# Cosformer attention into a top-1 mixture of experts: two lasting row tiles, a later one-hot table, earlier expert reads and copied row numbers

## The chip, the cores and the metric

The kernel runs on one core of one Trainium2 chip. The metric is the device time of one execution in microseconds, the median over runs; lower is better. Engines are named as the profile names them: PE (TensorE), DVE (VectorE), ACT (ScalarE), POOL (GpSimd), SP (SyncE). Transfers are issued by SP and POOL; the profile gives them as queue q1 (SP's) and q0 (POOL's).

## What is computed

```python
q_p = phi(q); k_p = phi(k)          # relu(x)*cos, relu(x)*sin: 64 -> 128 features
kv  = einsum('bhsf,bhsd->bhfd', k_p, v);  z = k_p.sum(axis=2)
x   = einsum('bhsf,bhfd->bhsd', q_p, kv) / (q_p . z + 1e-6)   # 8 x 8 x 576 x 64
x   = x.transpose(0, 2, 1, 3).reshape(4608, 512)
e_idx  = argmax(x @ w_gate)         # 8 experts, the best one alone
gate_w = softmax(x @ w_gate)[e_idx]; eom = sigmoid(x @ w_output_gate)
out[mask e] = gate_w * eom[:, e] * (relu(x[mask e] @ w1[e]) @ w2[e])   # 512 -> 1024 -> 512
```

## The kernel before

**Attention.** 36 units i = 0..35 of 128 rows, nine to a group g = 0..3 of two batches. PE multiplies a unit by the finished KᵀV (`q_mm`, L542, L547), ACT and DVE put it into a tile `u` (L554, L556), and after every second unit and after a group's last one `q_out` follows: DVE takes the reciprocal of the denominators (`rc`, L566, L567), POOL writes the divided rows as f16 into the group's `xr` tile (L576), and DVE (POOL for some) makes the gate products `gl` (L593) and sums them to gate numbers `glog` (L600). `xr` comes from a pool with two buffers, so group g takes the buffer of group g-2.

**Routing.** `route` (L607 to L667) is a generator that gives way at each `yield`; `step()` runs it on to the next one. It finds each row's expert (`ei`, L626), writes the one-hot table `oh` (L629), counts ranks within experts by six or ten small matmuls on PE (`rk`, L637, L639), and makes row numbers `di` and weights `meta` on DVE (to L666). Group 3 is routed in two halves, of slots 0 to 3 and 4 to 8 of the group. `scatter(g, c)` (L669) is POOL's: it copies `meta` behind the rows (L675), and an indirect DMA (L678) writes 128 rows to the table `xs`, sorted by expert, in HBM.

**Experts.** `xs` is worked off in 39 slots j of 128 rows of one expert; the first 8 (EARLY) take rows of groups 0 to 2 only. SP reads a slot (`fetch`, L811; `xg`, 8 buffers); PE turns it (`x_tr`, L824), ACT or DVE copies the turned tile (`xts`, L848); PE multiplies by the first matrix (`layer1`, L885, into `hp`), ACT applies relu (`hs`, L893); `h_tr` turns that again, by PE (L866) and a DVE copy (`hts`, L868) or, for slots 18 to 36, by a DMA of SP (L861); `products` (L907) multiplies by the second matrix into one of two halves of a PSUM tile `yps`; `output` scales it on DVE (`ysb`, L918, 5 buffers), and POOL writes 128 rows to the output by an indirect DMA (L922), the row numbers being those in `xg` (j < 8) or in `sidx`. `expert(j)` (L871) reads the expert's number into a register of PE's sequencer, by a load and two register instructions.

**Order.** The schedule is by hand: each engine runs its instructions in the order in which the code writes them, and waits there. Before the main loop stand slots 0 to 2 and the scatters of group 3; the main loop (L1152) does in iteration j: `h_tr(j-1)`, `x_tr(j+1)`, `expert(j+1)`, `layer1(j)`, `layer2` of slot j-1 (j-2 for the slots turned by DMA), the fetch of slot j+5. POOL also loads the experts' matrices (`load_w`, L238 and L241, 1 MB each in f16), those of ranks 4 to 7 in iterations 4 to 11. POOL's DMAs hold eight semaphores in turn (DMASW0 to DMASW7 in the listings below), so that an instruction that waits for one waits for a landing.

Of the kernel before, what the change touches and what calls it, by code (L numbers as in the profile page):

```python
# [13 lines left out]
I32 = mybir.dt.int32  # L14
U8 = mybir.dt.uint8
U16 = mybir.dt.uint16
# [6 lines left out]
def kernel(  # L23
# [237 lines left out]
    GP.memset(onesf[:], 1.0)  # L261
    valid = constp.tile([P, NL], U8, name="valid")
    sidx = constp.tile([P, NL], I32, name="sidx")
    GP.memset(sidx[:], BIG)
    nlate = constp.tile([P, 1], I32, name="nlate")
    perm = constp.tile([P, E, E], F32, name="perm")
# [7 lines left out]
    if True:  # L274


        zt = wk.tile([P, XW], U16, name="zt", tag="zt", bufs=1)
        DVE.memset(zt[:], 0)
        DVE.memset(zt[:, DM:DM + 2].bitcast(I32), BIG)

        def idle_mms(ps, n):

            z = zt[:, 0:DM].bitcast(F16)
            for _ in range(n):
                PE.matmul(ps, z[:, 0:P], z, start=True, stop=True)
# [324 lines left out]
        def route(g, glog, xrows, c0=0, c1=GC):  # L610


            m = c1 - c0
            lg = glog[:, c0:c1, 0:8]
            im8 = iota8m[:].unsqueeze(1).to_broadcast([P, m, E])
            lmax = small(f"lmax@{g}_{c0}", [P, m])
            DVE.tensor_reduce(lmax[:], lg, AX.X, ALU.max)
            lmb = lmax[:].unsqueeze(2).to_broadcast([P, m, E])
            sh = small(f"sh@{g}_{c0}", [P, m, E])
            DVE.tensor_tensor(sh[:], lg, lmb, ALU.subtract)  # L620
            om = small(f"oh@{g}_{c0}", [P, m, E])

            DVE.tensor_tensor(om[:], lg, lmb, ALU.is_equal)
            DVE.tensor_tensor(om[:], om[:], im8, ALU.mult)
            ei = small(f"ei@{g}_{c0}", [P, m])
            DVE.tensor_reduce(ei[:], om[:], AX.X, ALU.min)  # L626
            oh16 = oh16s[(m, g % 2)]
            oh = oh16[:, 0:m, :]
            DVE.tensor_tensor(oh, im8, ei[:].unsqueeze(2).to_broadcast([P, m, E]),  # L629
                              ALU.is_equal)  # L630
            yield
            ex = small(f"ex@{g}_{c0}", [P, m, E])
            ACT.activation(ex[:], sh[:], AF.Exp)

            rk_t = ptr.tile([P, 512], F32, name=f"rk{g}_{c0}", tag="tr")
            rk = rk_t[:, 0:(m + 1) * E].rearrange("p (c e) -> p c e", e=E)
            PE.matmul(rk, u16[:], oh16[:], start=True, stop=False)  # L637
            for c in range(m):
                PE.matmul(rk[:, c + 1:, :], ones16[:],  # L639
                          oh16[:, c:c + 1, :].to_broadcast([P, m - c, E]),  # L640
                          start=False, stop=(c == m - 1))
            ds_ = small(f"ds@{g}_{c0}", [P, m, E])
            DVE.tensor_tensor(ds_[:], rk[:, 0:m, :],
                              base[:].unsqueeze(1).to_broadcast([P, m, E]), ALU.add)
            DVE.tensor_tensor(base[:], base[:], rk[:, m, :], ALU.add)
            yield
            og = small(f"og@{g}_{c0}", [P, m, E])
            DVE.tensor_tensor(og[:], oh, glog[:, c0:c1, 8:16], ALU.mult)
            den = small(f"den@{g}_{c0}", [P, 2, m])
            DVE.tensor_reduce(den[:, 1, :], og[:], AX.X, ALU.add)  # L650
            yield
            ACT.activation(den[:, 1, :], den[:, 1, :], AF.Exp, scale=-1.0)
            yield
            DVE.tensor_tensor(ds_[:], ds_[:], oh, ALU.mult)
            df = small(f"df@{g}_{c0}", [P, m])
            DVE.tensor_reduce(df[:], ds_[:], AX.X, ALU.add)
            di = small(f"di@{g}_{c0}", [P, m], I32, bufs=5)
            DVE.tensor_copy(di[:], df[:])
            DVE.tensor_reduce(den[:, 0, :], ex[:], AX.X, ALU.add)
            DVE.tensor_scalar_add(den[:, 0, :], den[:, 0, :], 1e-9)  # L660
            meta = small(f"meta@{g}_{c0}", [P, m, 2], bufs=5)
            DVE.tensor_scalar(meta[:, :, 0].bitcast(I32), id0[:, c0:c1], float(2 * S * g),
                              None, ALU.add)
            DVE.scalar_tensor_tensor(den[:, 1, :], den[:, 1, :], 1.0, den[:, 0, :],
                                     ALU.add, ALU.mult)
            DVE.reciprocal(meta[:, :, 1], den[:, 1, :])  # L666
            scat[g] = (di, meta, xrows, c0, c1)  # L667
# [246 lines left out]
        def output(j):  # L914
            xg = xgs.pop(j)
            yp = yps[0][:, j % 2, :]
            ysb = fsb.tile([P, DM], F32, name=f"ysb{j}", tag="ysb", bufs=5)
            DVE.tensor_scalar(ysb[:], yp, xg[:, DM + 2:DM + 4].bitcast(F32),  # L918
                              None, ALU.mult)
            idx = (xg[:, DM:DM + 2].bitcast(I32) if j < EARLY  # L920
                   else sidx[:, j - EARLY:j - EARLY + 1])
            d = GP.indirect_dma_start(  # L922
                out=out[:, :],
                out_offset=bass.IndirectOffsetOnAxis(ap=idx, axis=0),
                in_=ysb[:], in_offset=None,
                bounds_check=N - 1, oob_is_err=False)
            tc.declare_no_dep(d.ins, group="so", reason="distinct rows")
            tc.add_to_no_dep_group("so", d.ins)
# [89 lines left out]
        for i, (b, c) in enumerate(units):  # L1018
            g = b // 2
            n = i % 9  # L1020
            if n == 0:
                glog = wk.tile([P, GC, 16], F32, name=f"glog{g}", tag="glog")
                xrows = wk.tile([P, GC, XW], U16, name=f"xr{g}", tag="xr")
                scd = 0
            if c % 2 == 0:
                u = u2[(g + n // 2) % 2]
# [29 lines left out]
            if 30 < i < NU - 2:  # L1056
                if i == 31:
                    ip = pkv.tile([P, 2, 512], F32, name="idle1", tag="kvp")
                idle_mms(ip[:, 0, :], 4)
            if i == NU - 3:  # L1060
                x_tr(0)
# [62 lines left out]
        late = late_table()  # L1124


        for j in range(3):
            expert(j)
        layer1(0, pkv.tile([P, 2, 512], F32, name="hp0", tag="kvp"))
        for x in range(4):  # L1130
            scatter(NG - 1, x)
# [3 lines left out]
        layer1(1)  # L1135
        h_tr(0)
        layer1(2)
        step()
        h_tr(1)
        expert(3)  # L1140
        x_tr(3)
        x_copy(3)
        step()
        products(0)
        products(1)
        step(2)
        assert not pending
        for x in range(4, GC):
            scatter(NG - 1, x)
# [2 lines left out]
        for j in range(3, NMAIN + 1):  # L1152
# [4 lines left out]

            for _ in range(3 if j < 5 else 0):
                next(late, None)
            if j + 1 < NMAIN:  # L1160
                expert(j + 1)
            if j < NMAIN:
                layer1(j)
            if j + 1 < EARLY:
                x_copy(j + 1)
            for m in (j - 2, j - 1):
                if (m in BY_DMA) == (m == j - 2):
                    if j == NMAIN - 1 and m == j - 1:

                        h_tr(j)  # L1170
                    layer2(m)
            if j == 6:
                late_valid()
            for jj in {4: [8, 9]}.get(j, [j + 5]):
                if 4 <= j and jj < NSLOT:
                    fetch(jj)
# [47 lines left out]
```

## Time and profile before

| what | value |
|---|---|
| median of 3 runs | 329.85 us (328.68 to 330.81) |
| profiled execution | 327.69 us, its span 326.0 us |
| PE busy | 290.2 us (89%) |
| DVE busy | 197.5 us (61%) |
| ACT busy | 157.1 us (48%) |
| POOL busy | 140.6 us (43%) |
| moved by DMA | 71.82 MB, mean 220 GB/s |
| queue q1, queue q0 | 43.1% and 38.6% of 16 DMA engines' span |

The profile is of one execution. Its span runs from the first instruction to the last; the execution's own time is 1.7 us longer. Shares are means over the whole span: attention ends at about 153 us, and the main loop runs from 171 us to the end, so the stretches are read one by one below. The page's own chain of the work that ended last holds nothing but the last output here, and is of no use.

### The profile page before, as it was taken

How to read it: one execution, taken by the hardware profiler on the slowest of the kernel's cores; microseconds unless marked ns; L12 is line 12 of the kernel's file. 1: busy time of each engine (PE TensorE's matmuls, PEld its weight loads, DVE VectorE, ACT ScalarE, POOL GpSimd, SP SyncE). 2: the span in 40 equal slices, each digit the busy share in tenths (PEclk: the TensorE clock that was granted, in tenths of full speed). 3: DMA queues.
4: the chain of work that ended last, by engine and by line, in shares of the span. 5: the costliest groups of instructions: out<-in, count | busy, mean ns of one | idle time of the engine just before them, and what ended most of it. 6: DMA issues, size and time to landing. Idle time of an engine off the chain costs nothing. (4 is left out here: it accounts for less than half of the span.)

```text
span 326.0 us, 9068 instructions
## 1 busy us (share of the span) xinstructions
PE 290.2 (89%) x3091; PEld 186.3 (57%) x3091; DVE 197.5 (61%) x536; ACT 157.1 (48%) x303; POOL 140.6 (43%) x184
## 2 busy tenths in 40 slices
PE   6879999999799789866789899998999999999982
PEld 2668787787688568645344455544554444444440
DVE  8545889876979999998958334443433322333231
ACT  4479798889968879525403232221223223222310
POOL 8003345368814885098677524342221322223222
PEclk9999999999979999999979999999999999999997
DMA  7999959585948399999992899999949887876621
GB/s 249 361 393 342 336 154 341 178 313 155 383 163 246 112 228 230 231 197 238 252 243 104 192 231 247 241 243 248 274 145 179 186 166 194 181 174 154 167 92 48
DMA packets 51037, 71.82 MB, mean 220 GB/s; under 512 B 23406, under 2 KB 30126, under 8 KB 49968
## 3 DMA queue, kind: packets, MB, share of 16 engines
q1 hardware_dynamic: 40608, 40.17, 43.1%
q0 software_dynamic: 10384, 31.05, 38.6%
q8 instruction: 28, 0.46, 0.6%
q14 instruction: 17, 0.14, 0.1%
HBM read 67.61 MB, written 16.17 MB: 257 GB/s over the span
## 5 line engine op out<-in xcount | busy, mean ns | idle before, releaser
L893 ACT ACTIVATE hs<-hp 128x1024 f16<-128x1024 f32 x39 | 39.9, 1024 | 112.5 <-PE hp L885 112.5
L918 DVE TENSOR_SCALAR ysb<-yps,xg 128x512 f32<-128x512 f32 x39 | 29.2, 750 | 85.5 <-PE yps L907 85.5
L885 PE MATMUL hp<-wt,xts 128*128 x312 | 73.8, 379 | 4.1 <-issue 4.0
L907 PE MATMUL yps<-wt,hts 128*128 x312 | 75.2, 385 | 1.3 <-DVE ysb L918 1.2
L922 POOL DMA_INDIRECT out_dram<-ysb,sidx x31 | 30.7, 990 | 83.6 <-DVE ysb L918 77.9
L907 PEld LDWEIGHTS <-hts 128*128 128x128 f16 x312 | 30.9, 99 | 39.4 <-issue 3.8
L542 PE MATMUL qo<-kvm,wt 64*128 64x162 f32 x512 | 45.3, 311 | 6.5 <-DVE wt L556 5.1
L885 PEld LDWEIGHTS <-xts 128*128 128x128 f16 x312 | 29.2, 98 | 32.6 <-issue 4.9
L554 ACT ACTIVATE wt<-qo,cosq 128x324 f32<-128x324 f32 x72 | 36.9, 530 | 17.1 <-PE qo L542 15.4
L542 PEld LDWEIGHTS qo<-kvm,wt 64*128 64x128 f32 x512 | 37.3, 186 | 12.2 <-DVE wt L556 7.8
L556 DVE SCALAR_TENSOR_TENSOR wt<-qo,sinq,wt 128x324 f32<-128x324 f32 x72 | 36.7, 548 | 10.6 <-ACT wt L554 8.1
L576 POOL TENSOR_TENSOR xr<-wt,rc 128x512 f16<-128x512 f32 x36 | 38.1, 1069 | 10.9 <-DMA xs<-xr,di@1_0_1651 10.6
L408 PE MATMUL kvp<-wt 64*64 64x132 f32 x1080 | 37.8, 279 | 5.4 <-ACT wt L359 1.6
L408 PEld LDWEIGHTS kvp<-wt 64*64 64x64 f32 x1080 | 30.4, 133 | 11.3 <-issue 4.6
L593 POOL TENSOR_TENSOR gl<-wt,rc 128x256 f32<-128x256 f32 x12 | 9.0, 751 | 51.5 <-DVE rc L567 20.3
L359 ACT ACTIVATE wt<-wt,tanc 128x256 f32<-128x256 f32 x57 | 25.8, 501 | 0.4 <-DVE wt L341 0.4
L508 ACT ACTIVATE qp<-wt 128x512 f32<-128x512 f32 x32 | 20.1, 632 | 8.5 <-PE qtp L520 4.5
L520 PE MATMUL qtp<-ident,qp 128*128 128x128 f32 x128 | 20.8, 287 | 0.0
L848 DVE COPY xts<-xtsp 128x512 f16<-128x512 f16 x31 | 13.0, 419 | 8.1 <-DMA wt<-in_moe_w_dram 2.5
L824 PE MATMUL xtsp<-ident,xg 128*128 128x128 f16 x156 | 14.9, 219 | 2.2 <-DMA xg<-xs 1.6
L520 PEld LDWEIGHTS qtp<-ident,qp 128*128 128x128 f32 x128 | 14.2, 146 | 4.2 <-issue 3.8
L350 ACT ACTIVATE wt<-wt,cosc 128x256 f32<-128x256 f32 x36 | 16.1, 496 | 0.0
(274 smaller groups left out, 333.8 us busy)
## 6 DMA issues: line engine op xcount, KB each, us to landing
wt<-in_moe_w_dram POOLq DMA_DIRECT2D x16, 1024.0 KB, 13.9
wt<-in_k_dram SPq DMA_DIRECT2D x16, 576.0 KB, 7.6
wt<-in_v_dram SPq DMA_DIRECT2D x16, 576.0 KB, 7.8
wt<-in_q_dram SPq DMA_DIRECT2D x16, 576.0 KB, 6.5
xg<-xs SPq DMA_DIRECT2D x43, 129.0 KB, 6.6
xs<-zt SPq DMA_DIRECT2D x9, 129.0 KB, 7.6
out_dram<-ysb,sidx POOLq DMA_INDIRECT x31, 3.2
hts<-hs SPq DMA_TRANSPOSE x19, 3.3
```

The source lines that it names most:

```text
L359: d = ACT.activation(t_, v_, AF.Copy, scale=tanc[:, c:c + 1])
L408: mm = PE.matmul(outs(i, mp), kcs[rows, m, c, :], mov, start=first, stop=(c == NCH - 1), skip_group_check=True)
L520: PE.transpose(toks(tp[:])[:, mh, :, l, :], qp[i % 2][:, at:at + 128], ident[:])
L542: PE.matmul(qo[:, 2 * mp + ih, 0:162], qT[r, hf, ih].rearrange("p l t -> p (l t)"), kvms[b][r, n0, :, :].rearrange("p w s -> p (w s)"), st ...
L554: d0 = ACT.activation(t, qs[:, :, :, 0], AF.Copy, scale=cosq[:, c:c + 1])
L556: d1 = DVE.scalar_tensor_tensor(u[:, h0:h0 + 4, :], qs[:, :, :, 1], sinq[:, c:c + 1], t, ALU.mult, ALU.add)
L576: GP.tensor_tensor(xrows[:, slot + x, 0:DM].bitcast(F16).rearrange("p (h d) -> p h d", d=D), u[:, 8 * x:8 * x + 8, 0:64], rc[:, 8 * x:8 * ...
L885: mm = PE.matmul(hp[:, fh * 512:fh * 512 + 512], xts[:, kc, :], wt[:, bass.ds(ev, 1), kc * F + fh * 512:kc * F + fh * 512 + 512], start=(k ...
L893: ACT.activation(hs[:].rearrange("p (c q) -> p c q", c=8), hp.rearrange("p (q c) -> p c q", c=8), AF.Relu)
L907: mm = PE.matmul(yp, hts[:, fc, :], wt[:, bass.ds(ev, 1), 4 * F + fc * DM:4 * F + fc * DM + DM], start=(fc == 0), stop=(fc == 7))
L918: DVE.tensor_scalar(ysb[:], yp, xg[:, DM + 2:DM + 4].bitcast(F32), None, ALU.mult)
L922: d = GP.indirect_dma_start(out=out[:, :], out_offset=bass.IndirectOffsetOnAxis(ap=idx, axis=0), in_=ysb[:], in_offset=None, bounds_check= ...
```

## The change

- The `xr` tiles become two tiles of their own that last for the whole kernel, used in turn by the groups. They are ordered by what is really written and read, row block by row block, and not as one buffer given back.
- In the second half of group 3's route a `yield` stands ahead of `oh`; the calls before the main loop are put in another order.
- The expert numbers of slots 0 to 3 are read in units 31 to 33, and those of slots 4 to 8 behind `layer1` of the slot before them and not ahead of it.
- `late_valid` (two small matmuls and the DVE instruction `valid`) stands ahead of `layer2` in iteration 6, not behind it.
- The row numbers of slots 0 to 7 are copied by DVE from `xg` into a tile `sidxe` (128x1, eight times), and the output's DMA reads them there.

```diff
+    sidxe = constp.tile([P, EARLY], I32, name="sidxe")
+        xrs = [wk.tile([P, GC, XW], U16, name=f"xr{x}", tag=f"xr{x}", bufs=1)
+               for x in range(2)]
@@ route @@
             DVE.tensor_reduce(ei[:], om[:], AX.X, ALU.min)
+            if g == NG - 1 and c0:
+                yield
             oh16 = oh16s[(m, g % 2)]
@@ output @@
+            if j < EARLY:
+                DVE.tensor_copy(sidxe[:, j:j + 1], xg[:, DM:DM + 2].bitcast(I32))
-            idx = (xg[:, DM:DM + 2].bitcast(I32) if j < EARLY
+            idx = (sidxe[:, j:j + 1] if j < EARLY
@@ units @@
-                xrows = wk.tile([P, GC, XW], U16, name=f"xr{g}", tag="xr")
+                xrows = xrs[g % 2]
             if 30 < i < NU - 2:
...
+                expert(i - 31)
+                if i == NU - 3:
+                    expert(3)
                 idle_mms(ip[:, 0, :], 4)
@@ before the main loop @@
-        for j in range(3):
-            expert(j)
         layer1(0, pkv.tile([P, 2, 512], F32, name="hp0", tag="kvp"))
...
         layer1(2)
-        step()
         h_tr(1)
-        expert(3)
-        x_tr(3)
-        x_copy(3)
         step()
         products(0)
+        x_tr(3)
+        step()
+        x_copy(3)
         products(1)
-        step(2)
+        step(3)
@@ main loop @@
-            if j + 1 < NMAIN:
+            if EARLY < j + 1 < NMAIN:
                 expert(j + 1)
             if j < NMAIN:
                 layer1(j)
+            if j + 1 <= EARLY:
+                expert(j + 1)
             if j + 1 < EARLY:
                 x_copy(j + 1)
+            if j == 6:
+                late_valid()
...
-            if j == 6:
-                late_valid()
```

The order on PE between `layer1(2)` and the second matrix of slot 1, before (`hs_2669` is slot 1's relu, `xg_2096` slot 3, `hts_2680` slot 0's turned tile):

```order
462 L885 MATMUL hp_2692<-wt,xts_2657 128x512
463 L637 LDWEIGHTS u_112
464 L637 MATMUL rk_4_2704<-oh_5_1_377,u_112 128x48
...
474 L639 MATMUL rk_4_2704<-oh_5_1_377,ones_113 128x8
475 L866 LDWEIGHTS hs_2669
...
491 L871 TENSOR_LOAD tab_139
492 L871 ISA x2
493 L824 LDWEIGHTS xg_2096
...
501 L907 LDWEIGHTS hts_2680
```

And of the change (`hs_2676` is slot 1's relu, `hts_2687` and `hts_2709` are the turned tiles of slots 0 and 1, `xg_2095` is slot 3):

```order
464 L890 MATMUL hp_2699<-wt,xts_2665 128x512
465 L871 LDWEIGHTS hs_2676
...
481 L912 LDWEIGHTS hts_2687
...
505 L829 LDWEIGHTS xg_2095
...
513 L642 LDWEIGHTS u_112
514 L642 MATMUL rk_4_2737<-oh_5_1_380,u_112 128x48
...
525 L912 LDWEIGHTS hts_2709
```

The rank matmuls `rk` went from ahead of everything behind `layer1(2)` to behind slot 0's second matrix and slot 3's turning, and the register load between went out.

The order on DVE from the last unit's experts on, before:

```order
355 L626 TENSOR_REDUCE ei@3_4_2666<-oh@3_4_2663 128x5
356 L629 TENSOR_TENSOR oh_5_1_377<-iota8m,ei@3_4_2666 128x40
357 L868 COPY hts_2680<-htsp_2681 128x1024
358 L643 TENSOR_TENSOR ds@3_4_2711<-rk_4_2704,base 128x40
359 L645 TENSOR_TENSOR base<-base,rk_4_2704 128x8
360 L868 COPY hts_2714<-htsp_2715 128x1024
```

And of the change:

```order
355 L629 TENSOR_REDUCE ei@3_4_2674<-oh@3_4_2671 128x5
356 L873 COPY hts_2687<-htsp_2688 128x1024
357 L873 COPY hts_2709<-htsp_2710 128x1024
358 L634 TENSOR_TENSOR oh_5_1_380<-iota8m,ei@3_4_2674 128x40
359 L648 TENSOR_TENSOR ds@3_4_2744<-rk_4_2737,base 128x40
360 L650 TENSOR_TENSOR base<-base,rk_4_2737 128x8
```

Both copies of turned tiles (slots 0 and 1) now stand ahead of the table `oh`.

The order on POOL where group 3's first rows are written, with waits, before (`xr_2053` is group 3's tile, `xr_1455` group 2's):

```order
111 L576 TENSOR_TENSOR xr_2053<-wt,rc_0_2266 128x512 [waits DMASW6_49,DMASW4_49,DMASW7_49,DMASW1_49,DVE_49]
112 L576 TENSOR_TENSOR xr_2053<-wt,rc_0_2266 128x512
113 L232 TENSOR_LOAD ordi
114 L232 ISA x2
115 L1219 ISA [waits wsem0,DMASW3_49]
```

And of the change:

```order
112 L579 TENSOR_TENSOR xr_168<-wt,rc_0_2265 128x512 [waits DVE_49]
113 L579 TENSOR_TENSOR xr_168<-wt,rc_0_2265 128x512
114 L232 TENSOR_LOAD ordi
115 L232 ISA x2
116 L1228 ISA [waits wsem0,DMASW3_49]
```

The first write waits for DVE's `rc` alone, and no longer for landings of group 1's scatters; what stands behind it is the same.

The order on SP at the fetch of slot 8, before:

```order
91 L814 DMA xg_3004<-xs 128x516 [waits DMASW1_49,DMAHW1_49,DMASW0_49,DVE_49]
```

And of the change:

```order
91 L819 DMA xg_3007<-xs 128x516 [waits DMAHW1_49,DMASW0_49,DVE_49]
```

One wait for a landing of POOL's went out; the fetches of slots 9 to 15 lose one each in the same way.

## Rows read from the trace of the kernel before

**Rows 1.** Who PE waited for, 175 to 222 us (total, times, longest, us)
```profile
PE hp L885 <- issue: 2.1, 5, 0.5
...
PE xtsp L824 <- DVE valid L764: 0.4, 1, 0.4
```
**Rows 2.** The same view of PE, 222 to 326 us
```profile
PE yps L907 <- DVE ysb L918: 1.2, 2, 0.8
```
**Rows 3.** Timeline of PE, 152 to 172 us: start, length, instruction, [idle before, releaser]
```profile
151.72 1.33 PE L547 MATMUL qo<-kvm,qTt 64*64 64x162 f32 x32 [0.82 <-DVE wt L556]
154.90 1.89 PE L885 MATMUL hp<-wt,xts 128*128 x8 [1.85 <-issue]
...
163.70 0.18 PE L637 MATMUL rk<-oh,u 128*128 128x48 f16 x1 [2.56 <-POOL xr L675]
...
165.28 5.30 PE L907 MATMUL yps<-wt,hts 128*128 x16
```
**Rows 4.** Timeline of DVE, 131 to 164 us
```profile
131.33 0.43 DVE L593 TENSOR_TENSOR gl<-wt,rc 128x256 f32<-128x256 f32 x1
...
139.33 0.94 DVE L593 TENSOR_TENSOR gl<-wt,rc 128x256 f32<-128x256 f32 x1
...
159.81 3.75 DVE L629 TENSOR_TENSOR oh<-iota8m,ei@3_4_2666 128x40 f16<-128x40 f32 x1
163.48 0.68 DVE L868 COPY hts<-htsp 128x1024 f16<-128x1024 f16 x1
```
**Rows 5.** Timeline of POOL, 136 to 183 us
```profile
137.93 2.05 POOL L576 TENSOR_TENSOR xr<-wt,rc 128x512 f16<-128x512 f32 x2 [10.57 <-DMA xs<-xr,di@1_0_1651]
...
160.43 3.06 POOL L576 TENSOR_TENSOR xr<-wt,rc 128x512 f16<-128x512 f32 x3
...
168.75 0.21 POOL L675 COPY xr<-meta@3_4_2791 128x10 f32<-128x10 f32 x1
...
171.65 0.97 POOL L678 DMA_INDIRECT xs<-xr,di@3_4_2787  x1 [1.42 <-DMA xs<-xr,di@2_0_2323]
...
182.39 0.80 POOL L238 DMA_DIRECT2D wt<-in_moe_w_dram  x1 [0.73 <-DMA xs<-xr,di@3_4_2787]
```
**Rows 6.** Busy time by stretch, one us: PEclk is the granted clock
```profile
166.00:167.00 1.00, 1.00 (x4) 0.30 (x2) 0.88 (x6) 0.17 (x2) 0.70 (x2) 0.50 0.87 197
```
**Rows 7.** Timeline of PE, main loop, 175 to 222.5 us
```profile
190.79 1.89 PE L885 MATMUL hp<-wt,xts 128*128 x8 [0.41 <-issue]
...
221.20 0.40 PE L824 MATMUL xtsp<-ident,xg 128*128 128x128 f16 x4 [1.59 <-DMA xg<-xs]
221.99 0.81 PE L885 MATMUL hp<-wt,xts 128*128 x3 [0.40 <-issue]
```
**Rows 8.** Who SP's queue waited for, 150 to 326 us
```profile
SPq L814 <- DMA out_dram<-ysb,xg: 23.4, 6, 7.7
```
**Rows 9.** Timeline of SP, 192.5 to 194 us: the fetch of slot 12
```profile
193.19 0.34 SPq L814 DMA_DIRECT2D xg<-xs  x1
```
**Rows 10.** Busy time by stretch; last three: PEclk, DMA share, GB/s
```profile
115.00:170.00 55.00, 43.52 (x518) 30.45 (x515) 48.28 (x136) 28.15 (x59) 37.40 (x43) 0.97 1.05 236
170.00:182.00 12.00, 11.06 (x78) 6.14 (x77) 8.67 (x30) 3.22 (x4) 8.10 (x9) 1.00 0.41 143
...
186.00:238.00 52.00, 49.24 (x328) 26.57 (x327) 21.01 (x45) 12.87 (x13) 16.05 (x19) 1.00 1.06 248
```
**Rows 11.** DMAs issued from 214.1 to 214.3 us: count, KB, us to landing
```profile
wt<-in_moe_w_dram POOLq DMA_DIRECT2D x1, 1024.0 KB, 22.2
...
out_dram<-ysb,sidx POOLq DMA_INDIRECT x1, 17.3
```
**Rows 12.** Timeline of DVE, 233 to 239 us: `ysb` of slots 15 and 16
```profile
233.89 0.75 DVE L918 TENSOR_SCALAR ysb<-yps,xg 128x512 f32<-128x512 f32 x1 [1.77 <-PE yps L907]
...
238.01 0.75 DVE L918 TENSOR_SCALAR ysb<-yps,xg 128x512 f32<-128x512 f32 x1 [1.77 <-PE yps L907]
```
**Rows 13.** Timeline of PE, 239 to 242 us: the second matrix of slot 17
```profile
240.21 1.89 PE L907 MATMUL yps<-wt,hts 128*128 x8
```

## Prediction

> **What bounds the kernel now.** I read the waits of PE by stretch first, since PE is the engine that is busy to the end. From 222 us on it waits for hardly anything (1.2 us) [rows 2]; between 175 and 222 us there are three small things: five pauses called "issue", 2.1 us, ahead of `layer1`, 0.4 us for `valid` [rows 1], and a wait of 1.59 us for a fetched slot [rows 7]. Between attention and the main loop it loses more: 1.85 us ahead of `layer1(0)`, 2.56 us ahead of `rk` [rows 3]. Behind that wait the clock is granted at 0.50 [rows 6], the lower of its two levels (1.2 against 2.4 GHz), so that the sixteen matmuls of slots 0 and 1 take 5.30 us where eight take 1.89 elsewhere [rows 3, 13]: some 1.5 us more than 3.78.
>
> Then I read POOL and the DMA share, because POOL carries scatters, outputs and weight loads in one queue. The DMA engines are full from 115 to 170 us (share 1.05) and from 186 to 238 us (1.06), and half empty between (0.41) [rows 10]. So there are two things to follow: PE's own work, on which the change gains plainly, and the transfers of ranks 4 to 7, which it hardly touches. The question is which of them sets the time at about slot 16; behind it PE runs without waits.
>
> **PE's side, part by part.**
>
> *Expert reads ahead of `layer1(0)`.* PE's attention ends at 151.72 + 1.33 = 153.05, `layer1(0)` starts at 154.90: 1.85 us, put down to "issue", that is to the three register reads [rows 3]. They move into units 31 to 33, where PE waits for DVE anyway ([rows 3] has such a wait of 0.82). I count them at nothing there; without that cover they would cost the 1.85 us again.
>
> *`oh` and the copies.* DVE starts `oh` at 159.81 and it takes 3.75 us, ending with POOL's three `xr` writes (160.43 + 3.06 = 163.49); only then comes the first copy `hts`, at 163.48 [rows 4, 5]. A row so long beside POOL's writes is a block, since the gate product `gl`, a kindred instruction, takes 0.43 us in one place and 0.94 beside POOL's write [rows 4, 5]. In the change both copies (0.68 each) go first: from 159.8 to 161.2. Slot 0's second matrix can start at about 160.6. `oh` still ends at about 163.6, as POOL's writes don't move (below), and `rk` and slot 1's matrix follow it: the latter ends near 163.6 + 0.5 + 1.9 = 166.0 in place of 165.28 + 5.30 = 170.58 [rows 3]. That is 4.6 us. PE's wait there shrinks to about 1.2 us, which I take not to lower the clock; if it does, 3.1 are left, and if `oh` slips in ahead of POOL, 6.
>
> The Trainium skill, page "SBUF — State Buffer", section "SBUF: two separate sides", says that VectorE and GpSimd share a port pair as an exclusive lock, held for a whole instruction, and that a VectorE instruction with two SBUF inputs is shut out by a GpSimd one that reads SBUF; the 3.75 us of `oh` agree. By the rule the copies, whose input is PSUM, run through; it also speaks against the first part of the change, since it would make the earlier `xr` write and DVE's `gl` of the same unit collide at each of the three units. By that the sum would lose up to 1.5 us of attention.
>
> From rows alone: `xr` of unit 28 now starts near 131.4, beside the `gl` at 131.33 (0.43), and no longer beside the one at 139.33 (0.94) [rows 4, 5]. What one place loses the other gains, 0.5 us; I take nothing, with 0.5 at each of the three units that end in DVE's `gl`, 1.5 us, either way as bounds. It would only shrink or swell PE's lead, which is cut short below.
>
> *Main loop.* The reads move behind `layer1` for slots 4 to 8. The pauses are 0.41 us ahead of `layer1` in [rows 7]; four of the five lie in slots 4 to 7, 1.7 of the 2.1 us [rows 1]. The reads are still made, now while matmuls are queued; I take 1.5 (0 to 1.7). `late_valid` ahead of `layer2` covers its 0.4 [rows 1].
>
> *`sidxe`.* SP waited 23.4 us in six fetches for outputs to land [rows 8]; that chain made the fetch of a slot late by 1.59 us at PE, with 0.40 behind it [rows 7]. The copy takes the landing out of it: 2.0 us. Eight copies of 128x1 cost DVE less than 0.3 us each, hidden in its waits of 1.77 us for PE [rows 12].
>
> PE's side together: 4.6 + 1.5 + 0.4 + 2.0 = 8.5 us at slot 15, with 5 to 10 as bounds.
>
> **The transfers' side.** POOL's wait of 10.57 us ahead of group 3's first `xr` goes [rows 5]. But POOL is stopped again by landings: at 171.65, for a scatter of group 2, which lands when the full queue gets to it, and behind it stand seven more indirect DMAs, one after the other, up to the load of rank 4 at 182.39 [rows 5]. A POOL that is earlier at 131 us changes none of that, since the DMA engines were full meanwhile [rows 10]. From there the loads of ranks 4 to 7 and the outputs between them share one queue. The last load takes 22.2 us and lands at about 236.4; the output issued just before it, slot 10's, takes 17.3 and lands at about 230.4 [rows 11]; slot 11's is issued behind the load and so lands at about 237 (my estimate, 236.4 to 237.9).
>
> `ysb` has five buffers: `ysb(15)` needs slot 10's output landed, `ysb(16)` slot 11's. They run at 233.89 and 238.01 [rows 12], so there are 3.5 and 1.0 us to spare before. A DVE that stops there holds the copy `hts` of the next slot behind it: 238.01 + 0.75 + 0.68 = 239.44, needed at 240.21 [rows 4, 12, 13], which leaves 0.8 us more. So PE can be earlier at slot 17 by no more than 1.0 + 0.8 = 1.8 us plus what the transfers themselves gain, s.
>
> For s: three or so fetches of 128 rows of 516 two-byte numbers, 132 KB, such as slot 12's at 193.19 [rows 9], which waited for landings [rows 8], fall into the half-empty stretch before 182 us. At 248 GB/s [rows 10] each frees 0.5 us: 1.6 us. One fetch more in the full stretch, since PE is ahead, takes 0.5 back, and a few tenths of gaps before 170 us close. I take s = 1.6 (0 to 3).
>
> So the 8.5 us shrink to 1.8 + 1.6 = 3.4. The rest becomes two new stops on PE, of some 2.5 us each, at the second matrices of slots 16 and 17. The stop of 2.56 us before was followed by the lower clock at a price of 1.5 us [rows 3, 6]; the first such price is covered by the second stop, the second is not. I charge 1.0 (0 to 1.5): 2.4 us are left. The profiled execution was 327.69 us, which gives 325.3; against the median of the runs, 329.85, it gives **327.4 us**.
>
> The Trainium skill, page "DMA: Bandwidth & Descriptors", section "Queues, rings and completion order", has each DMA engine take turns between queues, while the descriptors of one ring start in order. By that an output behind a load on POOL's queue waits for all of it, which the 17.3 us bear out; the sum by the rule is the same, and were outputs let past, the next rival's.
>
> **Rivals.**
>
> *The cap doesn't bind.* If slot 11's output lands early enough (loads issued earlier because POOL comes to them sooner, or an output that isn't held for the load ahead of it), most of PE's 8.5 us last, less the lower bound's doubts: I put it at 7.3, 322.5 us. For it: POOL is idle much of that time. Against it: the share of 1.06, and 17.3 us for an output of 256 KB.
>
> *Level.* s is near 0 and the lower clock comes in full: 1.8 - 1.5 = 0.3 us, 329.6. For it: the loads start where they started, 182.39, and every gap that PE's lead closes is filled by its own further fetches.
>
> *Slower.* `rk` now stands behind slot 0's second matrix, slot 3's turning and two copies, and the last five scatters wait for what comes out of it. POOL copies their `meta` at 168.75, behind four other scatters, and is held to 171.65 anyway [rows 5], so `meta` may come as late as about 170.5; I expect it where it was. If `rk` ran 3.5 us later than I think, POOL's chain, the load at 182.39 and the whole stream behind it would slip one for one, PE would wait for it at slot 17, and 6 us of delay would end at 333.5. Against it: PE is free when `oh` is done.
>
> **How the numbers follow.** About 1% (3.3 us) is what a measurement of this kernel can tell from no change. The forecast has 0.50, its own range 325.0 to 329.9 (s and the clock at their ends); no cap 0.26; level 0.15; slower 0.09. Faster than 326.6 is all of "no cap" and some 0.17 of the forecast: 0.43. Slower than 333.1 is most of the last, and a little noise: 0.08. Within 1% is the rest, 0.49. The range for 8 in 10 leaves out half of "no cap" and the slower case: 322.6 to 330.6.
>
> **What would show it.** In the changed profile: `layer1(0)` right behind attention; both `hts` copies at about 160 to 161 us and `oh` long still; clock 1.00 at 165 to 169 us; no wait for landings in SP's fetches 8 to 15; the load of rank 4 still at 182 us; then, as the point that decides, DVE's `ysb` of slots 15 and 16 waiting for landed outputs at 229 and 235 us, with PE stopped behind it. If those stops are absent and the time is near 322, the cap was wrong; if the load of rank 4 moves by more than 1 us either way, my reading of POOL was.

## The result

| kernel | median | lowest to highest | runs |
|---|---|---|---|
| before | 330.33 us | 328.68 to 331.63 | 4 |
| changed | 325.97 us | 323.71 to 327.30 | 4 |

The ratio is 0.988, with a 95% interval of 0.984 to 0.992: 4 us faster, where 2.4 were forecast (327.4, range 322.6 to 330.6). The profiled execution of the change took 323.71 us, its span is 322.1 us: 3.9 us less than before. In the experiments below, medians and ratios leave out executions that took over 1.5% longer than the fastest of the same kernel in the same lot.

**The transition.** The timeline of PE, changed kernel, 148 to 175 us (start, length, instruction; line numbers are up to nine higher than before):

```profile
151.31 1.90 PE L890 MATMUL hp<-wt,xts 128*128 x8
...
158.14 1.89 PE L912 MATMUL yps<-wt,hts 128*128 x8
...
160.22 0.18 PE L642 MATMUL rk<-oh,u 128*128 128x48 f16 x1
...
160.37 1.89 PE L912 MATMUL yps<-wt,hts 128*128 x8
...
162.76 1.89 PE L890 MATMUL hp<-wt,xts 128*128 x8
```

`layer1(0)` follows attention at once, at 151.31 in place of 154.90 [rows 3]; attention itself ends 1.7 us earlier, which I had not counted. The second matrices of slots 0 and 1 run apart, each in 1.89 us, so at the full clock, and the second ends at 162.26 in place of 170.58: 8.3 us, where I had worked out 4.6. What comes on top is POOL's and DVE's. DVE's timeline, 141 to 160 us, and POOL's, 129 to 180 us:

```profile
142.74 0.19 DVE L634 TENSOR_TENSOR oh<-iota8m,ei@3_0_2416 128x32 f16<-128x32 f32 x1
...
156.41 0.68 DVE L873 COPY hts<-htsp 128x1024 f16<-128x1024 f16 x1
158.34 0.69 DVE L873 COPY hts<-htsp 128x1024 f16<-128x1024 f16 x1 [1.25 <-PE htsp L871]
158.95 1.13 DVE L634 TENSOR_TENSOR oh<-iota8m,ei@3_4_2674 128x40 f16<-128x40 f32 x1
```

```profile
130.99 2.29 POOL L579 TENSOR_TENSOR xr<-wt,rc 128x512 f16<-128x512 f32 x2 [4.02 <-DVE rc L570]
...
156.94 3.07 POOL L579 TENSOR_TENSOR xr<-wt,rc 128x512 f16<-128x512 f32 x3
...
178.99 0.82 POOL L238 DMA_DIRECT2D wt<-in_moe_w_dram  x1
```

POOL's first `xr` write starts at 130.99 in place of 137.93, and all that follows on POOL is earlier too: the last three writes at 156.94 in place of 160.43, the load of rank 4 at 178.99 in place of 182.39 [rows 5]. I had said that it stays at 182. Both copies stand ahead of `oh`, as forecast, and `oh` is blocked for 1.13 us in place of 3.75 [rows 4].

**Where PE's lead went.** At slot 5 PE is 9.3 us ahead (`layer1` at 171.31; before 180.65). Then it stands still. PE's timeline, 170 to 190 us, and that of ACT and DVE:

```profile
171.31 1.89 PE L890 MATMUL hp<-wt,xts 128*128 x8
174.15 1.89 PE L912 MATMUL yps<-wt,hts 128*128 x8 [0.94 <-issue]
...
181.60 1.03 PE L871 MATMUL htsp<-ident,hs 128*128 128x128 f16 x8 [5.57 <-ACT hs L898]
...
182.85 3.62 PE L890 MATMUL hp<-wt,xts 128*128 x8
```

```profile
180.52 1.02 ACT L898 ACTIVATE hs<-hp 128x1024 f16<-128x1024 f32 x1 [9.67 <-remote]
...
180.62 0.75 DVE L925 TENSOR_SCALAR ysb<-yps,xg 128x512 f32<-128x512 f32 x1 [6.56 <-remote]
```

ACT's relu of slot 5 waits for PE's `layer1` alone, which ends at 171.31 + 1.89 = 173.20; it starts 7.3 us later. DVE's `ysb` waits for the matmuls that end at 176.04, and starts 4.6 us later. PE's signals are late: the trace records those that release the two only at 180.50 and 180.59 us, and PE in turn waits for what stood still. The matmuls behind the stop are at the lower clock (3.62 us for eight; granted clock 0.50 from 181 to 186 us). At slot 8 PE is 1.4 us ahead (193.55; before 194.91). The 2.0 us at slot 15's fetch are won as forecast: SP's fetches wait for no landed output any more, mostly for buffers ([rows 8] had 23.4 us for `out_dram`):

```profile
SPq L819 <- DVE ysb L925: 31.9, 11, 5.7
```

(SP's waits, 150 to 322 us: total, times, longest.) From there to the end the lead is 3.7 to 4.0 us. Between 188 and 252 us PE waits for nothing at all, and `ysb` waits for no output in this execution; that of slot 16, on DVE, waits for PE:

```profile
234.31 0.75 DVE L925 TENSOR_SCALAR ysb<-yps,xg 128x512 f32<-128x512 f32 x1 [1.54 <-PE yps L912]
```

So the stops that the prediction named as the deciding point are absent here, and the time is not near 322 either: in this execution the late signals took the lead that the landed outputs should have taken.

### The profile page after: what moved, and what is told of

Same layout as the page of the kernel before. It is cut to its first block, busy times and chain, and to the rows that moved or that the text cites. A ratio compares the mean times of both kernels' runs of the same rounds, so it can differ in the third digit from the quotient of the medians.

```text
span 322.1 us, 9070 instructions
## 1 busy us (share of the span) xinstructions
PE 290.4 (90%) x3091; PEld 186.2 (58%) x3091; DVE 191.8 (60%) x544; ACT 155.8 (48%) x303; POOL 140.8 (44%) x184
## 5 line engine op out<-in xcount | busy, mean ns | idle before, releaser
L912 PE MATMUL yps<-wt,hts 128*128 x312 | 74.2, 381 | 2.3 <-DVE ysb L925 1.2
L890 PE MATMUL hp<-wt,xts 128*128 x312 | 75.4, 385 | 0.4 <-DVE wt L559 0.4
L557 ACT ACTIVATE wt<-qo,cosq 128x324 f32<-128x324 f32 x72 | 36.2, 529 | 17.3 <-PE qo L545 10.9
L871 PE MATMUL htsp<-ident,hs 128*128 128x128 f16 x160 | 12.6, 223 | 5.6 <-ACT hs L898 5.6
L871 PEld LDWEIGHTS <-hs 128*128 128x128 f16 x160 | 10.9, 100 | 10.5 <-ACT hs L898 6.1
```

What stands on the lines that cost most here:

```text
L557: d0 = ACT.activation(t, qs[:, :, :, 0], AF.Copy, scale=cosq[:, c:c + 1])
L871: PE.transpose(hp16[:, fc * 128:(fc + 1) * 128], hs[:, fc * 128:(fc + 1) * 128], ident16[:, :])
L890: mm = PE.matmul(hp[:, fh * 512:fh * 512 + 512], xts[:, kc, :], wt[:, bass.ds(ev, 1), kc * F + fh * 512:kc * F + fh * 512 + 512], start=(k ...
L912: mm = PE.matmul(yp, hts[:, fc, :], wt[:, bass.ds(ev, 1), 4 * F + fc * DM:4 * F + fc * DM + DM], start=(fc == 0), stop=(fc == 7))
```

## The experiments

They ran in three lots, each on one chip, with the kernel before beside them (medians 330.47, 325.59 and 330.73 us). Times are to be compared within a lot; the runs of before scatter widely, so that the ratio differs somewhat from that of the medians. In lot 2 the changed kernel itself did not run.

| lot | kernel | median | ratio to before, 95% | rank 4 load | last load | `layer1(22)` | `ysb` waits for outputs |
|---|---|---|---|---|---|---|---|
| | before (page) | | | 182.39 | 214.16 | 251.96 | 0 |
| | changed (page) | | | 178.99 | 212.47 | 247.98 | 0 |
| 1 | again | 325.02 | 0.984 (0.979 to 0.988) | 182.17 | 213.78 | 249.13 | 5.8 |
| 1 | xrs_only | 327.51 | 0.994 (0.990 to 0.997) | 182.85 | 213.77 | 249.70 | 2.0 |
| 1 | no_xrs | 329.45 | 0.996 (0.993 to 0.999) | 184.99 | 218.38 | 253.28 | 6.1 |
| 1 | no_sidxe | 327.86 | 0.993 (0.988 to 0.997) | 183.85 | 214.82 | 252.18 | 0 |
| 2 | before_again (one run) | 328.38 | | 180.97 | 213.66 | 252.66 | 0 |
| 2 | no_order | 323.94 | 0.994 (0.990 to 0.999) | 180.13 | 213.62 | 248.29 | 9.8 |
| 2 | no_reads | 323.08 | 0.994 (0.990 to 0.998) | 178.99 | 213.44 | 248.81 | 13.6 |
| 2 | out03_sp | 318.79 | 0.984 (0.977 to 0.991) | 172.41 | 205.74 | 241.80 | 0 |
| 3 | again2 | 325.61 | 0.985 (0.980 to 0.991) | 183.35 | 215.08 | 250.12 | 2.7 |
| 3 | xrs_sidxe | 328.31 | 0.993 (0.989 to 0.998) | 182.00 | 216.26 | 251.19 | 2.8 |
| 3 | spread | 338.71 | 1.022 (1.014 to 1.030) | 182.59 | 260.68 | 247.60 | 0 |
| 3 | before_spread | 342.13 | 1.034 (1.026 to 1.041) | | | | |

The last four columns are from each kernel's profile, in us: the starts of POOL's first and last load from rank 4 on and of slot 22's first matrix, and what DVE's `ysb` waited for landed outputs between 190 and 250 us.

### Lot 1: is the stop of the change, and what are the tiles and the copy worth

**again** is the changed kernel.

> The changed kernel itself, once more, with a profile of another execution. In the profile at hand PE is 9.3 us ahead at slot 5's layer1 (171.31 against 180.65) and then stands 5.6 us, while ACT and DVE stand 9.7 and 6.6 us behind it; 1.4 us of the lead are left at slot 8. Theory S1, the change itself brings the stop (a read of an expert number behind layer1, or something that waits for a transfer): it is there again, 4 us or longer between 170 and 185 us, and the ratio to the kernel before is about 0.988. Theory S2, a chance event of that one execution: no stop of more than 1 us there; then PE keeps about 9 us at slot 8, and what bounds it comes later, at ysb of slots 15 and 16 by my forecast; the ratio still 0.985 to 0.992 if that cap binds at 3.4 us, about 0.975 if nothing binds.

There is a stop again, 4.1 us on PE between 176 and 181 us, and the ratio is near that of the result: S1 by its numbers, though not by its cause, since the late signals come with kernels that lack the change as well (last section). The waits of PE, 150 to 326 us, and DVE's timeline, 229 to 237 us:

```profile
PE yps L912 <- DVE sidxe L923: 4.1, 1, 4.1
...
PE yps L912 <- DVE hts L873: 1.2, 1, 1.2
```

```profile
229.90 0.75 DVE L925 TENSOR_SCALAR ysb<-yps,xg 128x512 f32<-128x512 f32 x1 [1.92 <-DMA out_dram<-ysb,sidx]
235.99 0.75 DVE L925 TENSOR_SCALAR ysb<-yps,xg 128x512 f32<-128x512 f32 x1 [3.85 <-DMA out_dram<-ysb,sidx]
```

The second row of the waits is new: DVE's copy `hts` behind a `ysb` that waits for an output. The two `ysb` are those of slots 15 and 16, and PE stops behind the second. This is the sign that the prediction named, in the changed kernel itself, but small: PE's lead over the page of before shrinks from 4.1 us at slot 14 (217.86; 221.99) to 2.8 at slot 22.

**xrs_only**: before, with `xrows = xrs[g % 2]` and the two lasting tiles.

> The kernel before with the two lasting xr tiles alone. Theory of the prediction: POOL is earlier at 131 us, but the load of rank 4 stays at 182.4 us and the time stays, ratio 0.997 to 1.003. Theory T1, from the profile of the change: POOL's earlier writes let its DMAs be issued earlier, the DMA engines, though busy, then move more, and the load of rank 4 comes at 179 to 180.5 us; oh is blocked less long or earlier, layer1(0) starts 1.5 to 2 us earlier; ratio 0.988 to 0.995, that is a good part of the gain.

The ratio, 0.994, lies in T1's range and not in mine, and `layer1(0)` is 2.1 us earlier (152.78). The load of rank 4 is not earlier here (182.85). In this profile it stands behind slot 3's output on POOL, and that behind a second matrix of slot 3 that PE could start only at 176.6, at the lower clock, after late signals (timelines of PE and POOL, 163 to 187 us):

```profile
176.63 3.27 PE L909 MATMUL yps<-wt,hts 128*128 x8 [2.77 <-DVE so@l L741]
...
180.97 0.98 POOL L924 DMA_INDIRECT out_dram<-ysb,xg  x1 [4.38 <-DVE ysb L920]
```

**no_xrs**: the change, with `xrows = wk.tile(..., tag="xr")` again.

> The change without the lasting xr tiles (the pool with two buffers again), all else as changed. Theory of the prediction: nothing is lost, ratio to the kernel before 0.986 to 0.991, load of rank 4 at 182 to 183 us either way. Theory T1: load of rank 4 back at about 182.4, first xr of group 3 waiting about 10 us again, slot 1's second matrix ending near 166 in place of 162.3; the time loses 1.5 to 3 us against the change, ratio 0.993 to 0.997.

4.4 us slower than again. POOL's first write is back at 138.21, the last load 4.6 us later than in again (218.38 against 213.78), `layer1(22)` 4.2 us later. T1 holds, with more than its 3 us. The tiles are worth 4.4 us of the change's 5.4 in this lot when taken away, and 2 (by the ratio) to 3 (by the medians) when alone. Through which wait is not shown: xrs_only gains, and its load of rank 4 is no earlier than on the page of before.

**no_sidxe**: the change without the `tensor_copy` to `sidxe`, the DMA reading `xg`.

> The change without the copied row numbers: the fetches of slots 8 to 15 wait for landed outputs again, about 23 us in six fetches on SP. If these waits cost PE time, as in the kernel before (1.6 us for slot 15 and 0.4 behind it, or earlier slots now that PE is ahead), the ratio to the kernel before is 0.993 to 1.0, 2 us or more worse than the change; if the outputs' landings bound the end anyway (the cap of the prediction), no worse than 0.991.

2.8 us slower than again; the ratio, 0.9925, lies at the lower edge of the first branch. SP waits 23.7 us for outputs in five fetches, and PE 1.0 us plus 0.4 for the fetch of slot 15. From the last load's issue to `layer1(22)` it is 37.4 us, against 35.4 in again: 2.0, the term of the prediction.

### Lot 2: late signals, order, reads, and POOL's row of DMAs

**before_again** is the kernel before.

> The kernel before, with a profile of another execution. In the profiles of the change and of the three variants PE's signals reach the engines that wait for them late between about 162 and 182 us (ACT's relu of slot 5 starts 2.8 to 7.3 us after the matmul that it waits for, and PE's lead over the kernel before, 5 to 9 us at slot 3 or 4, is nearly used up by slot 7); in the profile of before there is no such lateness at all. Theory L1, the lateness belongs to POOL issuing DMAs one behind the other, whatever the kernel: it is there in this profile too, with stops of PE of 2 us or more in all between 165 and 190 us, and layer1 of slot 7 starts later than 190.8. Theory L2, it comes only when PE is early: none here, layer1 of slot 7 within 0.7 us of 190.8.

No late signals, in it or in the three others of this lot: L1 fell. L2 falls too: PE is early in all three of those, and none of them has late signals. Its number is wrong as well, since slot 7's `layer1` is at 184.81, 6.0 us earlier than on the page, without any edit. It bought nothing in this one run, which is among the longer ones of before in this lot. The waits of PE, 150 to 326 us:

```profile
PE hp L885 <- issue: 4.5, 8, 1.6
PE xtsp L824 <- DMA xg<-xs: 4.2, 2, 3.8
```

The second row, waits for fetched slots, is 1.6 us on the page of before. By slot 15 the 6.0 us are gone (226.69; page 226.11), and the last load was issued within 0.5 us of the page's.

**no_order**: the change without the `yield` ahead of `oh`, and with the calls of before (`rk` ahead of `h_tr(1)`).

> The change without its new order: oh ahead of both copies of turned tiles on DVE again, rk ahead of slot 1's turning on PE; all else as changed. Theory of the prediction: the order carries most of the gain at the transition; slot 3's layer1 starts 3 us or more later than 162.7, and the ratio to the kernel before is 0.990 to 0.996. Theory B: with the lasting tiles oh would start at 156.4, ahead of POOL's three writes at 156.9, and isn't blocked; slot 3's layer1 within 1 us of 162.7 and the ratio as with the change, 0.982 to 0.988.

The timeline of PE, 152 to 172 us:

```profile
162.24 0.18 PE L640 MATMUL rk<-oh,u 128*128 128x48 f16 x1 [2.62 <-DVE oh L632]
...
163.73 4.97 PE L910 MATMUL yps<-wt,hts 128*128 x16
...
169.21 1.89 PE L888 MATMUL hp<-wt,xts 128*128 x8
```

The wait for `oh` and the slow sixteen matmuls of [rows 3] are back, and slot 3's `layer1` starts at 169.21, 4.8 to 6.6 us later than in the three profiles of the change: the prediction's branch, not theory B's. The changed kernel did not run beside it, so its price in time is not measured. In the main loop PE's lead over the page of before shrinks from 6.9 us at slot 14 (215.10) to 3.7 at slot 22, where `ysb` of slots 14 to 16 waits for outputs.

**no_reads**: the change with `expert(0..3)` and `expert(j + 1)` where they were before.

> The change without the earlier reads of expert numbers: three reads stand ahead of layer1(0) again, one ahead of slot 3's turning, and those of slots 4 to 8 ahead of layer1. If they cost PE their time: layer1(0) 1.8 us later, pauses of 0.4 ahead of layer1 of slots 4 to 7, ratio to the kernel before 0.989 to 0.994. If the stop between 165 and 185 us swallows whatever PE gains before it: slot 7's layer1 within 0.7 us of the change's 189.0 to 189.4, ratio 0.982 to 0.988.

`layer1(0)` starts at 153.57, but this time it waits 1.42 us for a fetched slot; the pauses in the main loop are 0.3 us. The ratio is at the upper edge of the first branch, slot 7's `layer1` (184.81) fits neither, and the change did not run beside it, so what the reads alone are worth stays open. Its profile shows something better. DVE's timeline, 212 to 240 us, and PE's, 218 to 242 us:

```profile
217.70 0.75 DVE L925 TENSOR_SCALAR ysb<-yps,xg 128x512 f32<-128x512 f32 x1 [1.80 <-DMA out_dram<-ysb,sidx]
223.75 0.75 DVE L925 TENSOR_SCALAR ysb<-yps,xg 128x512 f32<-128x512 f32 x1 [4.06 <-DMA out_dram<-ysb,sidx]
229.91 0.75 DVE L925 TENSOR_SCALAR ysb<-yps,xg 128x512 f32<-128x512 f32 x1 [4.21 <-DMA out_dram<-ysb,sidx]
235.60 0.75 DVE L925 TENSOR_SCALAR ysb<-yps,xg 128x512 f32<-128x512 f32 x1 [3.54 <-DMA out_dram<-ysb,sidx]
```

```profile
225.25 1.89 PE L912 MATMUL yps<-wt,hts 128*128 x8 [1.45 <-DVE hts L873]
...
231.41 1.89 PE L912 MATMUL yps<-wt,hts 128*128 x8 [1.88 <-DVE hts L873]
...
237.10 1.89 PE L912 MATMUL yps<-wt,hts 128*128 x8 [1.41 <-DVE hts L873]
```

This is the cap that the prediction described, in its place and two slots earlier as well: `ysb` of slots 13 to 16 waits for landed outputs (the expectation of again2 calls them 14 to 17), the copy `hts` behind it is late, and PE stands at the second matrices of slots 15 to 17. PE was 8.3 us ahead of the page of before at slot 14 (213.67; 221.99) and is 3.1 ahead at slot 22. The eight matmuls behind each stop take 1.89 us, at a granted clock of 1.00: the clock did not fall after stops of 1.4 to 1.9 us.

**out03_sp**: the change, with this in `output` (cut; `side` is a tensor in HBM), which leaves the first four slots' rows out of the result:

```python
            if j < 4:
                SP.dma_start(side[j * P:(j + 1) * P, :], ysb[:])
                return
```

> The change with the outputs of slots 0 to 3 written by SP as plain rows to a side tensor, so that those four slots' rows are left out of the result. POOL has four indirect DMAs less, 5.2 us of issuing, at the end of its row of ten. Theory L1 (late signals belong to POOL's issuing, or to waits for it): PE's signals come on time from about 175 us on instead of 180 to 181, the load of rank 4 starts at 174 to 177 us instead of 179 to 182, slot 7's layer1 starts at about 184 to 186 instead of 189, and the ratio to the kernel before is 0.970 to 0.978. Rival, the stop has another cause (late table, fetches of slots 8 and up, a DMA that lands): slot 7's layer1 stays within 1 us of 189 and the ratio at 0.982 to 0.988.

With signals on time in this lot, L1 could not be tried by it, and slot 7 (181.96) is earlier than either branch had it. For the cap it is the clearest run: the load of rank 4 is at 172.41, 6.6 us earlier than in no_reads, the last load 7.7 us earlier, no `ysb` waits for an output, PE's lead over the page of before is 9.8 us at slot 14 (212.16) and 10.2 at slot 22, `layer1(22)` is 7.0 us earlier than in no_reads and the median 4.3 us lower, although PE stands 2.6 us at slot 8 for a fetched slot. It is no clean pair with no_reads: the reads differ as well. And its ratio to before, 0.984, is no better than the change's in the other lots, since the kernel before is itself some 5 us faster in this one.

### Lot 3: the cap taken away, and two parts alone

**again2** is the changed kernel once more.

> The changed kernel a third time, beside the three below. In the profile of no_reads, where PE's signals were on time, DVE's ysb waited four times for landed outputs (1.8, 4.1, 4.2, 3.5 us, slots 14 to 17) and PE stood 1.45, 1.88 and 1.41 us behind it: the cap of the prediction. If the change is bound by it, this profile shows the same waits if PE is 5 us or more ahead at slot 14; ratio to the kernel before 0.983 to 0.990.

The signals are late again, PE is only 2.5 us ahead of the page of before at slot 14, and `ysb` waits once, 2.7 us, for an output.

**spread**: the change, with

```diff
-        wload = {4: [(4, 0)], 5: [(4, 1)], 6: [(5, 0)], 7: [(5, 1)],
-                 8: [(6, 0)], 9: [(6, 1)], 10: [(7, 0)], 11: [(7, 1)]}
+        wload = {4: [(4, 0)], 5: [(4, 1)], 8: [(5, 0)], 10: [(5, 1)],
+                 13: [(6, 0)], 16: [(6, 1)], 19: [(7, 0)], 22: [(7, 1)]}
...
```

and with each slot from 22 on waiting for its own expert's matrices, in place of one wait for all.

> The change with the loads of ranks 5 to 7 spread over iterations 8 to 22 in place of 6 to 11 (the wait for all loads at slot 22 replaced by each slot's own wait, by its table, as slots 8 to 21 have it), so that the queue isn't full and outputs don't stand behind loads. If the landed outputs are the cap: no waits of ysb for outputs, PE keeps the lead it has at slot 12 (5 to 9 us over the kernel before) to the end; ratio 0.968 to 0.980, 2 to 5 us better than again2. Rival, the lead is lost elsewhere (late signals, loads that come too late for rank 5 to 7): ratio within 0.004 of again2, or worse.

To slot 22 it does what the cap theory says: no wait of `ysb` for an output, `layer1(22)` at 247.60 in place of 250.12 (again2). Then it loses far more: 13.1 us against again2 by the medians. The waits of PE, 150 to 345 us:

```profile
PE yps L912 <- DMA hts<-hs: 12.2, 3, 5.9
```

From slot 18 on `h_tr` is a DMA of SP's. Two loads now fall there (issued at 240.78 and 260.68), and the long waits for transposes end at 254.8 and 273.4, 5.9 us the longest; the matmuls behind them are slow too (3.4 to 3.6 us for eight). That the loads hold the transposes up is read from the times alone. So the early, crowded loads of the kernel may well serve it, by keeping the queues free for the transposes.

**before_spread**: the same edit in the kernel before.

> The kernel before with the same spread loads. If the cap binds only a PE that is early, as the prediction says (1.0 us to spare before), this gains no more than the wait for fetched slots that came late behind outputs: ratio 0.990 to 1.001. Rival, the full queue of loads slows the kernel before as well: 0.980 to 0.989.

Slower as well (1.034), and PE waits for the transposes in the same way, so it says nothing on whether the kernel before was capped.

**xrs_sidxe**: before, with the tiles and the copy alone.

> The kernel before with two parts alone, the lasting tiles and the copied row numbers; neither the new order nor the earlier reads. If the cap binds the change, what order and reads win on PE (3 to 4 us) is lost again at slots 15 to 17 and the ratio is within 0.004 of again2. Rival, no cap: 2 to 4 us slower than again2, ratio 0.991 to 0.997.

2.7 us slower than again2, so the rival's number: order and reads are worth something after all, although the cap, by my expectation, should have taken it. From the last load to `layer1(22)` it is 34.9 us, as in again2 (35.0); what differs is when the last load is issued, 1.2 us later. So the gain of order and reads may come through the start of the stream of loads, but a profile of each explains only 1.1 of the 2.7 us, and the rest is open.

## Why the prediction was right, and where not

**The cap is there.** In the seven profiles in which `ysb` waited for outputs, slot 22's `layer1` starts 34.7 to 35.9 us behind the issue of the last load (again 35.4, xrs_only 35.9, no_xrs 34.9, no_order 34.7, no_reads 35.4, again2 35.0, xrs_sidxe 34.9; differences of the table), although slot 8 had started anywhere between 188.93 and 196.61. In both profiles of the kernel before it is 37.8 and 39.0. That alone is no proof, since the page of the change (35.5) and out03_sp (36.1) are near it without any such wait. Closer to the mechanism is `ysb` of slot 16, which needs slot 11's output, the first behind the last load: in all seven it waits for a landing and starts 21.5 to 22.7 us behind that load's issue; the prediction had 22.2 for the load's own landing. What it takes shows where signals were on time: of PE's lead 8.3 us became 3.1 in no_reads and 6.9 became 3.7 in no_order, while out03_sp, with its stream earlier, kept all.

**But it is not what shaped the measured time.** In no profile of the change did PE come to slot 15 with the 8.5 us worked out. The late signals, which the prediction does not have, left it 1.4, 1.8 and 0.5 us ahead of the page of before at slot 8 (page of the change, again, again2), and the fetch gave back 2.0 to 2.3. The cap then took nothing, 1.2 and 0.5 us (PE's waits for `hts` between 188 and 252 us). In the page of the change `ysb` of slot 16 ran 21.8 us behind the last load's issue, so just where the cap would have stopped it. One loss stood in for another, and left nearly the same lead: that is luck, and so, in part, is the nearness of 325.97 to 327.4.

Nor is page against page like against like: the page of before has its signals on time. `layer1(22)` of again and again2 is 2.8 and 1.8 us earlier than there, but their medians are 5.4 and 5.1 us below those of before beside them. No profile of the kernel before itself shows what it loses where signals are late, so how the 5 us of lots 1 and 3 are made up stays open; what the change is worth where signals are on time was not measured.

**The terms.** From the page of before to that of the change `layer1(22)` gained 251.96 - 247.98 = 4.0 us: 1.7 by an earlier last load (214.16 to 212.47; my s, 1.6), and 2.3 behind it (37.8 to 35.5; my 1.8). This splits a difference and shows no cause, as no `ysb` waited there; and in again and again2 the last load came 0.4 us earlier and 0.9 us later than on the page of before: that s fits is luck too. The third term, 1.0 us less for a clock that falls behind the two stops, was mis-sized: where the stops came (no_reads) they were 1.4 to 1.9 us, not 2.5, and cost no clock. 1.8 + 1.6 without it is 3.4, against the 4 measured.

**What failed.** First, the step "a POOL that is earlier at 131 us changes none of that, since the DMA engines were full meanwhile". A share of 1.05 is not a rate. From 138 to 150 us the two kernels' rows are (before, then changed; last three: clock, DMA share, GB/s)

```profile
138.00:150.00 12.00, 9.25 (x91) 6.43 (x90) 11.62 (x26) 4.35 (x10) 10.59 (x13) 1.00 1.03 212
```

```profile
138.00:150.00 12.00, 9.97 (x99) 6.92 (x95) 10.83 (x29) 5.81 (x13) 10.15 (x11) 1.00 1.07 237
```

at nearly the same share 12% more is moved, with other transfers in the stretch (6% over 130 to 155 us: 224 and 237 GB/s). I had costed the lasting tiles at nothing; taking them away cost 4.4 us. They also end blocks on DVE that I had not priced: `oh` of the first half takes 0.19 us, where before it took 1.71 beside POOL's write of 144.58, and attention ends 1.7 us earlier. DVE's timeline of before:

```profile
144.00 1.71 DVE L629 TENSOR_TENSOR oh<-iota8m,ei@3_0_2408 128x32 f16<-128x32 f32 x1
```

Second, the stops at the second matrices of slots 16 and 17 are not in the page of the change, and in again there is one, of 1.2 us: the lead was spent before, at 173 to 190 us, by late signals, which no trace of before had shown. That the load of rank 4 "moves by more than 1 us" I had named as the sign that my reading of POOL was wrong, and so it was.

**Right.** `layer1(0)` behind attention; both copies ahead of `oh`; the full clock at 160 to 169 us; SP's waits for outputs gone, worth 2.0 us; the 0.4 us for `valid` gone, though never tried alone; the small price for the early `xr` beside `gl`. The collision of these two that the prediction feared came out mildly: DVE's `gl` started first and took 0.43 us, and POOL's two writes took 2.29 us where they took 2.05. By the Trainium skill, page "SBUF — State Buffer", section "SBUF: two separate sides", the one that starts first keeps the shared ports for its whole instruction; these rows agree (0.24 us longer behind a `gl` of 0.43). The Trainium skill, page "DMA: Bandwidth & Descriptors", section "Queues, rings and completion order", has the descriptors of a ring consumed in order. The trace of no_reads agrees: slot 11's output, issued 0.9 us behind the last load (214.32; 213.44), landed 0.8 us behind it (235.51; 234.72).

**Rivals.** "The cap doesn't bind" is out where signals were on time, by no_reads, no_order and out03_sp. Where they were late it is half true: the cap took 1.2 us at most from the change, and xrs_sidxe came out the rival's way. "Level" and "slower" did not come: `meta` of the last five slots was ready at 162.6, earlier than POOL wanted it.

## What to carry to other kernels

When one engine is made earlier, look for the stream that it doesn't carry (here weight loads and outputs in one queue), and for the buffers that tie it to that stream: in no_reads and no_order its gain ended there, and in out03_sp, which starts the stream earlier, it was kept. A full DMA share does not say that earlier issue is worthless; compare the rate. And a tile pool's rotation can make one write wait for a whole group's transfers: tiles that last, ordered by what is really read, were the largest part of this change where its parts were measured (4.4 of 5.4 us). And a time near the forecast does not show that the forecast's path was taken: compare the profiles at the place where it says the time is lost.

The next step that these runs point to is to start the stream earlier, as out03_sp does by taking four outputs from ahead of the load of rank 4. A kernel with the right result that does so was not run.

## What had not been expected of the hardware

Signals of PE, ACT and DVE can reach the engines that wait for them late, several at once: ACT's relu of slots 3 to 5 starts up to 7.3 us behind the matmuls that it waits for (8.2 in before_spread). This is so in all profiles of lots 1 and 3 and in that of the change, and it costs PE most between 162 and 182 us; in lot 2 and on the page of before no relu of the first twelve slots starts more than 0.6 us late. It goes with the lot and not with the kernel, as xrs_only and before_spread have it too. In the change's trace about 100 of 1050 signals of DVE, ACT and PE have no record within 0.15 us of the instruction that gives them, from 72 us on, and some 70% of these fall into POOL's issuing of DMAs, which holds 28% of all signals; before has none. Not all of these need be late: of DVE's 509 signals 446 have a record at all. The medians of before are 330.5 and 330.7 us in the lots with late signals and 325.6 in the other. Whether the chip, the recording of the profile or something else sets it was not settled, and no run took POOL's issuing away where signals were late.
